# Second layers of expert pairs on four 32-column tiles of TensorE, gathers first, other weight buffers: attention and mixture of experts on one core

## The chip, the core and the metric

One core of a Trainium2 chip runs the whole program. The metric is the device time of one execution in microseconds (us), less is better. TensorE (PE) multiplies, VectorE (DVE) and ScalarE (ACT) work on rows in the on-chip memory and read the products out of PSUM, GpSimd (POOL) issues the indirect DMAs, and SyncE (SP) issues the plain DMAs of this stage. All DMAs of the core share 16 DMA engines.

## The reference

Attention with normalised queries and keys makes 3584 rows of 768 numbers. A gate picks one of 8 experts for each row, each expert keeps at most 80 rows, and those go through two layers. All other rows of the output are zero.

```python
q_n, k_n = rmsnorm(q, g_q), rmsnorm(k, g_k)        # batch 8, heads 12, seq 448, head_dim 64
attn = softmax(q_n @ k_n.T / 8);  x = attn @ v     # as (3584, 768)
logits = x @ w_gate                                # 8 experts
expert_idx = argmax(logits);  gate_w = softmax(logits)[expert_idx]
for e in range(8):
    tok_idx = the rows with expert_idx == e, the 80 of largest gate_w if there are more
    h = np.maximum(x[tok_idx] @ w1[e], 0.0)        # 768 x 1024
    out[tok_idx] = gate_w[tok_idx, None] * (h @ w2[e])   # 1024 x 768
```

## The kernel before

**Attention.** The 96 heads are done in 24 groups of four. Scores (L408) and products with v (L425) run on PE as four 64x64 tiles of the array at once, in f32, in an order written out by hand as slots. The gate's sums (L460) run as eight tiles of 64 rows by 32 columns. While this goes on, POOL copies the weights of experts 3 to 7 into a scratch in DRAM as bf16 (`stage_w`), and loads those of experts 0 to 2 on the chip.

**Late weights.** Near the end of attention SP begins to load the weights of experts 3 to 5 from the scratch into the memory that attention gives back (`weights_early`, `weights_late`, `fetch_late`). A weight tile that lies over a buffer of attention waits until that buffer has been read for the last time. Of expert 5, w1 is issued after the routing of the last batch has begun (L919 and the line behind it: a small memset holds it back), and w2 when the first gathered rows are there (L1023, again a memset that holds it back). Experts 6 and 7 go into the slots of experts 0 and 1 when PE is done with those (last two lines). SP works through its list in order, so a transfer that waits holds those behind it.

**Routing of the last batch.** DVE, PE and ACT find which rows each expert keeps, up to the indices `idxG`. PE fills its pauses with products that nobody reads (`busy`).

**Experts.** `gather(e)` fetches 80 rows by an indirect DMA. There are four row buffers, so gathers 0 to 3 are issued at once and gather e + 4 after the rows of e have been used. `xpose(e)` divides the rows by their softmax sums (three DVE products, L1017), transposes them on PE (six, L1027) and copies them out (DVE, L1030). The first layer is 48 matmuls with w1 as the stationary operand and 80 columns moving (L1045), and ACT's Relu (L1049). The second layer is 16 matmuls with 80 columns of h stationary and 384 columns of w2 moving (L1076): 8 chunks of the hidden size times two halves of the output. DVE weights the two halves (L1082) and POOL scatters the 80 rows to the output (L1064). The experts follow each other on PE, each as first layer, transposes of the next expert's rows, second layer. The last expert's output goes out in two scatters.

Of the kernel before, what the change touches and what calls it, by code (L numbers as in the profile page):

```python
# [21 lines left out]
def kernel(  # L22
# [154 lines left out]
    beat = tpool.tile([128, NJ + 1, 512], BF16, name="beat")  # L177
# [69 lines left out]
    vpool = av_stack.enter_context(tc.tile_pool(name="vp", bufs=3))  # L247
    apool = av_stack.enter_context(tc.tile_pool(name="attn", bufs=6))
    qktpool = av_stack.enter_context(tc.tile_pool(name="qkT", bufs=2))
    smpool = av_stack.enter_context(tc.tile_pool(name="sm", bufs=4))  # L250
    with av_stack:
# [24 lines left out]
        def load_v(g):  # L276
            vt = vpool.tile([128, NB, D], F32, tag="v", name="vt")
            load(g, vt, v, nc.sync)
            st[g]["v"] = vt
# [67 lines left out]
        def keys_turned(n):  # L347
# [5 lines left out]
            T = qktpool.tile([128, 2, S], F32, tag="qkT1", name="qkT")  # L353
# [26 lines left out]
        def transp(g, a):  # L380
# [6 lines left out]
            T = qktpool.tile([128, 2, S], F32, tag=f"qkT{a}", name="qkT")  # L387
# [531 lines left out]
    nc.vector.memset(w_tiles[NW0 + 2][0][0][:, 0, 0:2], 0.0)  # L919
    fetch_late(NW0 + 2, (0, ))  # L920
# [61 lines left out]
    def gather(e, wait=False):  # L982

        if e % 4 == 3:
            xgs[e] = prep.tile([128, NJ + 1, 256], F32, tag="xb", name="xg")[
                :CAP].rearrange("p j d -> p (j d)")[:, :XW]
        else:
            xgs[e] = upool.tile([128, 2, S], F32, tag="us", name="xg")[:CAP].rearrange(
                "p u s -> p (u s)")[:, :XW]
        if wait:  # L990
            nc.vector.memset(xgs[e][:, 0:1], 0.0)
        nc.gpsimd.indirect_dma_start(
            out=xgs[e], out_offset=None, in_=xr_dram[:, :],
# [18 lines left out]
    def xpose(e):  # L1012
        xg = xgs[e]
        xn = mpool.tile([CAP, DM], BF16, tag="xn", name="xn")
        for i in range(NQ):
            c = slice(256 * i, 256 * i + 256)
            nc.vector.tensor_mul(  # L1017
                xn[:, c].rearrange("p (hh u d) -> p u hh d", hh=2, u=2),
# [3 lines left out]
            if e == 0 and i == 0:  # L1022
                nc.vector.memset(w_tiles[NW0 + 2][1][0][:, 0, 0:2], 0.0)  # L1023
                fetch_late(NW0 + 2, (1, ))
        pxt = mps.tile([128, DC, CAP], BF16, tag="pxt", name="pxt", bufs=1)
        for c in range(DC):
            nc.tensor.transpose(pxt[:, c, :], xn[:, c * 128:(c + 1) * 128],  # L1027
                                identb[:CAP, :CAP])
        xgT = mpool.tile([128, DC, CAP], BF16, tag="xgT", name="xgT")
        nc.vector.tensor_copy(xgT[:], pxt[:])  # L1030
        xts[e] = xgT

    for e in range(1, 4):
        gather(e)
    xpose(0)

    busy(2)
    for e in range(E):
        h_sb = mpool.tile([128, FC, CAP], BF16, tag="hsb", name="h_sb")
        for fh in range(2):  # L1040
            ph = mps.tile([128, FC // 2, CAP], F32, tag="ph", name="ph")
            for f4 in range(FC // 2):
                fc = fh * (FC // 2) + f4
                for c in range(DC):
# [4 lines left out]
            nc.scalar.activation(h_sb[:, fh * (FC // 2):(fh + 1) * (FC // 2), :],  # L1049
                                 ph[:], AF.Relu)  # L1050
        if e + 1 < E:
            xpose(e + 1)
        if e < E - 4:
            gather(e + 4, wait=True)
        DN = DM // 2
        yo = mpool.tile([CAP, DM], F32, tag="yo", name="yo", bufs=3)

        def scatter(half=None):
            if half is None:
                o, at, y, n = outs[e], idxT[:, e:e + 1], yo[:, :], N  # L1060
            else:
                o = outs[e + half].rearrange("n (h d) -> (n h) d", h=2)
                at, y, n = idxL[:, half:half + 1], yo[:, half * DN:half * DN + DN], 2 * N
            nc.gpsimd.indirect_dma_start(  # L1064
                out=o[:, :], out_offset=bass.IndirectOffsetOnAxis(ap=at, axis=0),
# [77 lines left out]
```

## Time and profile before

| | us |
|---|---|
| three runs | 414.49, 417.03, 416.99 |
| median of them | 416.99 |
| profiled execution, its own time | 414.97 |
| span of its trace, first to last instruction | 413.3 |
| PE busy | 398.7 (96%) |
| DVE busy | 355.3 (86%) |
| ACT busy | 314.0 (76%) |
| attention and routing, up to the first matmul of an expert | 370.8 |
| experts, from there to the end | 42.5 |

The span is cut from the first to the last instruction of the program, so the execution's own time is 1.67 us more. Busy times are sums over the whole span, and the stages have different limits: what the table says of PE as a whole doesn't say what bounds the last 42.5 us.

### The profile page before, as it was taken

Reading aid. Unit: us, or ns where it says so; the run is one execution under the profiler, and the core shown is the slowest. Engines: PE = TensorE matmul, PEld = TensorE weight load, DVE = VectorE, ACT = ScalarE, POOL = GpSimd, SP = SyncE. Lnnn points to the kernel's source line nnn. Section 1 sums busy time; section 2 is a strip of 40 time slices with the busy share of each in tenths; the row PEclk is TensorE's granted clock in tenths of the full one; section 3 lists DMA queues with packets and bytes.
Section 4 is the critical chain, followed back from the end, with each engine's and each line's share of the span. In section 5 each row is a group of like instructions: output and inputs, shape, how many; then the busy total and the mean of one; then the engine's idle time right before and its main releaser. Section 6 shows DMA issues by size and latency. Waiting matters only on the chain.

```text
span 413.3 us, 12608 instructions
## 1 busy us (share of the span) xinstructions
PE 398.7 (96%) x5293; PEld 195.6 (47%) x5293; DVE 355.3 (86%) x659; ACT 314.0 (76%) x480; POOL 88.8 (21%) x148
## 2 busy tenths in 40 slices
PE   8999999999999999999999999999999999889994
PEld 7344444444444445344444444444344443448883
DVE  4999887998999999988999999989999969745551
ACT  5898979997989799979899699978997784502211
POOL 6200002501040013221241025111502030134422
PEclk9999999999999999999999999999999999999999
DMA  7459999999989899989999999999899285989991
GB/s 240 142 157 210 274 305 231 272 209 304 253 222 275 230 251 277 290 183 255 244 290 247 229 271 257 268 227 303 210 231 299 58 309 195 253 237 341 355 315 48
DMA packets 76072, 100.92 MB, mean 244 GB/s; under 512 B 8416, under 2 KB 65248, under 8 KB 76016
## 3 DMA queue, kind: packets, MB, share of 16 engines
q1 hardware_dynamic: 59856, 70.53, 53.2%
q0 software_dynamic: 15872, 29.13, 38.7%
q8 instruction: 41, 0.67, 0.6%
q10 hardware_dynamic: 288, 0.46, 0.4%
q14 instruction: 15, 0.12, 0.1%
HBM read 101.11 MB, written 39.89 MB: 341 GB/s over the span
## 4 chain that ended last, share of the span: by engine, by line
PE 84%; DVE 5%; ACT 5%; issue 2%; POOL 1%; DMA 1%; POOLq 0%; DVEq 0%
PE ps L408 31%; PE po L425 28%; PE zl L460 5%; PE py L1076 5%; PE tp L366 4%; PE ph L1045 4%; PE xp L366 3%; ACT at L411 1%; DVE sm L443 1%; DVE qn L329 1%; DVE ms L299 1%; DMA xg<-xr_scratch,idxG 1%; PE mp L638 1%; ACT zsb L470 1%; ACT zo L472 1%
## 5 line engine op out<-in xcount | busy, mean ns | idle before, releaser
L408 PE MATMUL ps<-qkT 64*64 64x448 f32 x1344 | 147.6, 548 | 2.8 <-ACT row L592 1.3
L411 ACT ACTIVATE at<-ps 128x896 f32<-128x896 f32 x168 | 146.5, 930 | 4.5 <-PE ps L408 3.3
L425 PE MATMUL po<-at,vt 64*64 64x448 f32 x1344 | 142.5, 537 | 0.0
L443 DVE TENSOR_TENSOR sm<-sm,at 128x896 f32<-128x896 f32 x120 | 130.5, 1088 | 3.1
L425 PEld LDWEIGHTS po<-at,vt 64*64 64x64 f32 x1344 | 50.0, 133 | 74.0 <-issue 63.9
L408 PEld LDWEIGHTS ps<-qkT 64*64 64x64 f32 x1344 | 43.5, 132 | 67.5 <-issue 26.3
L299 DVE TENSOR_REDUCE ms<-sq 128x14 f32<-128x896 f32 (+1 forms) x50 | 51.9, 1041 | 7.1 <-ACT sq L292 7.0
L329 DVE TENSOR_TENSOR qn<-qk,rs 128x896 f32<-128x896 f32 (+1 forms) x47 | 50.5, 1077 | 1.6 <-issue 0.3
L292 ACT ACTIVATE sq<-qk 128x896 f32<-128x896 f32 (+1 forms) x48 | 44.5, 930 | 2.1 <-DMA qk<-in_q_dram 2.1
L216 POOL COPY mark<-mark 1x1 bf16<-1x1 bf16 x22 | 7.9, 359 | 138.9 <-DVE mark L215 138.9
L1049 ACT ACTIVATE h_sb<-ph 128x320 bf16<-128x320 f32 x16 | 7.0, 438 | 38.0 <-PE ph L1045 32.4
L705 ACT COPY xb<-xp 128x1024 f32<-128x1024 f32 x24 | 24.3, 1012 | 8.8 <-PE xp L366 8.4
L366 PEld LDWEIGHTS tp<-ident,qn 64*128 64x128 f32 x672 | 23.5, 139 | 12.6 <-issue 4.4
L366 PE MATMUL tp<-ident,qn 64*128 64x64 f32 x672 | 27.1, 226 | 0.6 <-POOL qn L329 0.4
L432 ACT COPY us<-po 128x896 f32<-128x896 f32 (+1 forms) x24 | 21.4, 894 | 6.5 <-PE po L425 6.4
L441 DVE TENSOR_TENSOR sm<-at 128x896 f32<-128x896 f32 x24 | 26.0, 1083 | 0.1
L395 ACT ACTIVATE qkT<-tp,gqk 128x896 f32<-128x896 f32 x23 | 23.6, 1026 | 0.0
L397 ACT COPY qkT<-tp 128x896 f32<-128x896 f32 x24 | 22.0, 916 | 2.0 <-PE tp L366 2.0
L1076 PE MATMUL py<-w_sb,h_sb 128*80 128x384 bf16 (+1 forms) x136 | 22.4, 317 | 0.1
L460 PE MATMUL zl<-us,wgs 64*32 64x448 f32 x192 | 20.4, 540 | 0.0
L460 PE MATMUL zl<-sm,zsel 64*32 64x448 f32 x192 | 20.3, 540 | 0.0
L366 PEld LDWEIGHTS xp<-ident,us 64*128 64x128 f32 x384 | 14.0, 139 | 12.0 <-ACT at L411 10.6
(185 smaller groups left out, 426.0 us busy)
## 6 DMA issues: line engine op xcount, KB each, us to landing
wb_scratch<-in_moe_w_dram POOLq DMA_DIRECT2D x20, 768.0 KB, 10.2
w_sb<-wb_scratch SPq DMA_DIRECT2D x9, 1536.0 KB, 13.6
vt<-in_v_dram SPq DMA_DIRECT2D x24, 448.0 KB, 6.5
out_dram<-zeros SPq DMA_DIRECT2D x28, 384.0 KB, 6.5
qk<-in_q_dram SPq DMA_DIRECT2D x23, 448.0 KB, 7.3
qk<-in_k_dram SPq DMA_DIRECT2D x23, 448.0 KB, 5.5
w_sb<-in_moe_w_dram POOLq DMA_DIRECT2D x6, 1536.0 KB, 15.7
xr_scratch<-xb SPq DMA_DIRECT2D x48, 192.0 KB, 7.1
```

The source lines that it names most:

```text
L292: nc.scalar.activation(o, x, AF.Square)
L299: nc.vector.reduce_sum(out=st[g]["ms"][:, a, lo:hi], in_=st[g]["sq%d" % a][:, lo:hi], axis=AX.X)
L329: e.tensor_mul(qn[:].rearrange("p (x hh) d -> p hh x d", hh=2)[:, h0:h1], qk[:, lo:hi].rearrange("p (hh x) d -> p hh x d", x=NX), rs[:, lo ...
L366: nc.tensor.transpose(o, w, one[p, p], tile_position=(p.start, 0))
L408: nc.tensor.matmul(ps[u * 64:u * 64 + 64, hh, :S], T1[d, u, x * 64:(x + 1) * 64], T0[d, u, :], start=True, stop=True)
L411: nc.scalar.activation(at[:], ps[:, :, :S], AF.Exp)
L425: nc.tensor.matmul(po[u][hh * D:(hh + 1) * D, u, :S], vt[p, hh * NX + x, :], at[p, hh, :], start=(x == 0), stop=(x == RD - 1))
L441: nc.vector.tensor_add(s["sm"][:], s["at0"][:], s["at1"][:])
L443: nc.vector.tensor_add(s["sm"][:], s["sm"][:], s["at%d" % x][:])
L460: nc.tensor.matmul(t[32 * c:32 * c + 32, r, :S], w, x, start=(i == 0), stop=(i == NQ - 1))
L705: nc.scalar.copy(xb[:].rearrange("p j (u hh d) -> p hh (j u) d", u=2, hh=2), xp[:].rearrange("p hh (k d) -> p hh k d", d=D))
L1076: nc.tensor.matmul(py[:, :c1 - c0], h_sb[:, fc, :], chunk(e, 1, fc)[:, c0:c1], start=(fc == 0), stop=(fc == FC - 1))
```

## The change

Four things change in the expert stage, and one in the layout of memory. Expert 0 and expert 7 keep their second layer. Experts 1 to 6 go in pairs (1,2), (3,4), (5,6): both first layers, then `second_layers`. That makes three products of 384 columns, each into one PSUM bank: the 80 rows of one half of one expert's output as column tiles of 32, 32 and 16 columns of the array at PSUM partitions 0 to 79, and in the fourth column tile, at partitions 96 and up, a third of the rows of the fourth half (expert b, second half). ACT weights what is in the fourth tile, with a copy of the gate weights at those partitions (`gwL`). There are six row buffers: gathers 0 to 5 are issued at once, and gathers 6 and 7 right after the rows of experts 0 and 1 have been divided. The division (`normal`) is issued two experts ahead of use, in `turn_rows(e)` for expert e + 2. Expert 7's slot is refilled after the second layers of the pair (1,2). The buffers of attention are laid out so that w2 of expert 4 lies over buffers of the last group but one, and w1 of expert 5 is issued in `weights_late` without a memset.

```diff
-    vpool = av_stack.enter_context(tc.tile_pool(name="vp", bufs=3))
+    vpools, qktpools = [], []
+    for last in range(2):
+        vpools.append(av_stack.enter_context(tc.tile_pool(name=f"vp{last}", bufs=2 - last)))
+        qktpools.append(av_stack.enter_context(tc.tile_pool(name=f"qkT{last}", bufs=1)))
...
             fetch_late(NW0 + 1)
+            fetch_late(NW0 + 2, (0, ))
...
-    nc.vector.memset(w_tiles[NW0 + 2][0][0][:, 0, 0:2], 0.0)
-    fetch_late(NW0 + 2, (0, ))
...
+    def gather(e):
+        if e == 5:
+            t = tpool.tile([128, XW], F32, tag="beat", name="xg")[:CAP]
+        elif e in (3, 4):
+            t = prep.tile([128, NJ + 1, 256], F32, tag="xb", name="xg")[
...
+    def turn_rows(e):
         pxt = mps.tile([128, DC, CAP], BF16, tag="pxt", name="pxt", bufs=1)
...
+        xts[e] = mpool.tile([128, DC, CAP], BF16, tag="xgT", name="xgT")
+        nc.vector.tensor_copy(xts[e][:], pxt[:])
+        if e + 2 < E and e:
+            normal(e + 2)
...
+    TB = [slice(32 * t, min(32 * t + 32, CAP)) for t in range(3)]
+    lasts = [slice(96, 96 + t.stop - t.start) for t in TB]
+    def second_layers(a, b):
+        rows_of(a)
+        rows_of(b)
+        for k, (e, half) in enumerate(((a, 0), (a, 1), (b, 0))):
+            py = product(k)
+            last = lasts[k]
+            for fc in range(FC):
+                for p in TB:
+                    nc.tensor.matmul(py[p, :], hs[e][:, fc, p],
+                                     chunk(e, 1, fc)[:, half * DN:half * DN + DN],
+                                     start=(fc == 0), stop=(fc == FC - 1))
+                nc.tensor.matmul(py[last, :], hs[b][:, fc, TB[k]], chunk(b, 1, fc)[:, DN:],
+                                 start=(fc == 0), stop=(fc == FC - 1))
+            weighted(yos[e][:, half * DN:half * DN + DN], py[:CAP, :], gwT[:, e:e + 1], False)
+            weighted(yos[b][TB[k], DN:], py[last, :], gwL[last, k, b:b + 1], True)
+            if k:
+                scatter(e)
+
+    for e in range(1, 6):
+        gather(e)
+    normal(0)
+    turn_rows(0)
+    normal(1)
+    normal(2)
+    for e in range(6, E):
+        gather(e)
+    busy(2)
+    first_layer(0)
...
+    turn_rows(1)
+    second_layer(0, lambda: turn_rows(2))
+    refill(0)
+    for a in range(1, E - 1, 2):
+        first_layer(a)
+        turn_rows(a + 2)
+        first_layer(a + 1)
+        if a + 3 < E:
+            turn_rows(a + 3)
+        second_layers(a, a + 1)
+        if a == 1:
+            refill(1)
+    first_layer(E - 1)
+    second_layer(E - 1)
```

The order of DVE, from the division of expert 0's rows to the weighting of expert 1's output. `xn` are divided rows, `xgT` transposed ones, `yo` weighted output. Before:

```order
L1017 TENSOR_TENSOR xn<-xg 80x2x2x64 x2
L1030 COPY xgT<-pxt 128x480
L1017 TENSOR_TENSOR xn<-xg 80x2x2x64 x3
L1030 COPY xgT<-pxt 128x480
L991 MEMSET xg 80x1
L1082 TENSOR_SCALAR yo<-py,gwT 80x384 x2
L1017 TENSOR_TENSOR xn<-xg 80x2x2x64 x3
L1030 COPY xgT<-pxt 128x480
L991 MEMSET xg 80x1
L1082 TENSOR_SCALAR yo<-py,gwT 80x384 x2
```

The same engine and place with the change, up to the copy of expert 4's rows:

```order
L1021 TENSOR_TENSOR xn_5807<-xg_5763 80x2x2x64 x2
L1036 COPY xgT_5820<-pxt_5813 128x480
L1021 TENSOR_TENSOR xn_5822<-xg_5797 80x2x2x64 x3
L1021 TENSOR_TENSOR xn_5826<-xg_5799 80x2x2x64 x3
L1036 COPY xgT_5899<-pxt_5892 128x480
L1021 TENSOR_TENSOR xn_5901<-xg_5801 80x2x2x64 x3
L1036 COPY xgT_5923<-pxt_5916 128x480
L1021 TENSOR_TENSOR xn_5925<-xg_5803 80x2x2x64 x3
L1084 TENSOR_SCALAR yo_5905<-py_5906,gwT_5767 80x384
L1084 TENSOR_SCALAR yo_5905<-py_5907,gwT_5767 80x384
L1036 COPY xgT_6006<-pxt_5999 128x480
L1021 TENSOR_TENSOR xn_6008<-xg_5805 80x2x2x64 x3
```

The divisions of experts 2, 3 and 4 now stand ahead of the weighting of expert 0, and each division (xg_5799 is gather 2, xg_5801 gather 3, xg_5803 gather 4, xg_5805 gather 5) stands ahead of the copy of the transposed rows of an earlier expert.

The list of SP from the last w1 part of expert 4 to the end. `xb` and `rz` are the attention's rows and their softmax sums on the way to DRAM, where the gathers read them. Before:

```order
L231 DMA w_sb<-wb_scratch 128x1024
L229 DMA w_sb<-wb_scratch 128x8x768
L717 DMA xr_scratch<-xb 64x3x256 x2
...
L509 DMA xr_scratch<-rz 64x3x12
L229 DMA w_sb<-wb_scratch 128x6x1024
L229 DMA w_sb<-wb_scratch 128x8x768
L229 DMA w_sb<-wb_scratch 128x6x1024
L229 DMA w_sb<-wb_scratch 128x8x768
L229 DMA w_sb<-wb_scratch 128x6x1024
L229 DMA w_sb<-wb_scratch 128x8x768
```

The same list with the change:

```order
L231 DMA w_sb<-wb_scratch 128x1024
L229 DMA w_sb<-wb_scratch 128x8x768
L229 DMA w_sb<-wb_scratch 128x6x1024
L719 DMA xr_scratch<-xb 64x3x256 x2
...
L511 DMA xr_scratch<-rz 64x3x12
L229 DMA w_sb<-wb_scratch 128x8x768
L229 DMA w_sb<-wb_scratch 128x6x1024
L229 DMA w_sb<-wb_scratch 128x8x768
L229 DMA w_sb<-wb_scratch 128x6x1024
L229 DMA w_sb<-wb_scratch 128x8x768
```

One transfer has moved, w1 of expert 5 (128x6x1024): it stands ahead of the last rows of attention now and no longer behind the last softmax sums. The five behind it (w2 of expert 5, then w1 and w2 of experts 6 and 7) keep their order.

## Rows read from the trace of the kernel before

**Rows 1.** Busy time by stretch: PE, PEld, DVE, ACT, POOL, clock, DMA share, GB/s

```profile
366.00:371.00 5.00, 4.18 (x28) 1.78 (x26) 1.81 (x6) 0.00 (x0) 3.20 (x4) 1.00 0.68 179
371.00:401.00 30.00, 30.00 (x479) 25.22 (x477) 17.02 (x44) 6.08 (x14) 10.63 (x10) 1.00 1.04 347
401.00:402.00 1.00, 1.00 (x8) 0.73 (x7) 0.10 (x1) 0.05 (x1) 0.00 (x0) 1.00 0.67 212
402.00:403.00 1.00, 1.00 (x13) 0.75 (x12) 0.66 (x2) 0.00 (x0) 0.00 (x0) 1.00 0.11 45
```

**Rows 2.** The chain of work that ended last, in the expert stage: start, us

```profile
365.41 3.42 DMA xg<-xr_scratch,idxG
370.80 1.88 PE ph L1045 x48
372.90 2.60 PE py L1076 x16
375.50 1.72 PE ph L1045 x48
```

**Rows 3.** Timeline of PE over the experts: start, us, count

```profile
372.52 0.38 PE L1027 MATMUL pxt<-identb,xn 80*128 80x80 bf16 x6
372.74 2.77 PE L1076 MATMUL py<-w_sb,h_sb 128*80 128x384 bf16 x16
375.34 1.88 PE L1045 MATMUL ph<-xgT,w_sb 128*128 128x80 bf16 x48
...
402.76 1.88 PE L1045 MATMUL ph<-xgT,w_sb 128*128 128x80 bf16 x48
404.48 3.07 PE L1076 MATMUL py<-w_sb,h_sb 128*80 128x384 bf16 x24
```

**Rows 4.** Timeline of PE at the gate's sums, first matmul of two batches

```profile
348.36 0.54 PE L460 MATMUL zl<-sm,zsel 64*32 64x448 f32 x1
...
348.73 0.54 PE L460 MATMUL zl<-sm,zsel 64*32 64x448 f32 x1
```

**Rows 5.** Timeline of PE at the start: f32 on the whole array

```profile
6.23 1.91 PE L852 MATMUL wps<-zeros 128*128 128x192 f32 x10
```

**Rows 6.** Timeline of SP: w2 of expert 4, w1 and w2 of 5

```profile
351.44 0.37 SPq L229 DMA_DIRECT2D w_sb<-wb_scratch  x1
359.50 0.48 SPq L229 DMA_DIRECT2D w_sb<-wb_scratch  x1
369.32 0.36 SPq L229 DMA_DIRECT2D w_sb<-wb_scratch  x1
```

**Rows 7.** Timeline of POOL: gathers 2 and 3, scatter of expert 5

```profile
368.01 0.90 POOL L992 DMA_INDIRECT xg<-xr_scratch,idxG  x1 [0.30 <-issue]
369.21 0.90 POOL L992 DMA_INDIRECT xg<-xr_scratch,idxG  x1 [0.30 <-issue]
...
399.22 0.91 POOL L1064 DMA_INDIRECT out_dram<-yo,idxT  x1 [3.35 <-DVE yo L1082]
```

**Rows 8.** DMA issues, gathers 3 and 4: the last number is us to landing

```profile
xg<-xr_scratch,idxG POOLq DMA_INDIRECT x1, 7.5
xg<-xr_scratch,idxG POOLq DMA_INDIRECT x1, 7.9
```

**Rows 9.** Timeline of DVE: experts 0 and 1, division of expert 3's rows

```profile
370.67 1.08 DVE L1017 TENSOR_TENSOR xn<-xg 80x256 bf16<-80x256 f32 x3
372.94 0.41 DVE L1030 COPY xgT<-pxt 128x480 bf16<-128x480 bf16 x1 [1.19 <-PE pxt L1027]
...
374.89 1.26 DVE L1082 TENSOR_SCALAR yo<-py,gwT 80x384 f32<-80x384 f32 x2 [1.54 <-PE py L1076]
...
380.63 1.08 DVE L1017 TENSOR_TENSOR xn<-xg 80x256 bf16<-80x256 f32 x3
```

**Rows 10.** Timeline of SP and DMA issues: w2 of expert 7, us to landing

```profile
382.27 4.47 SPq L229 DMA_DIRECT2D w_sb<-wb_scratch  x1
...
w_sb<-wb_scratch SPq DMA_DIRECT2D x1, 1536.0 KB, 20.3
```

More of the change, by code (lines that the diff above doesn't have):

```diff
@@ L175 @@
                             compare_op=ALU.is_gt, fill=0.0, base=0, channel_multiplier=-1)
-    beat = tpool.tile([128, NJ + 1, 512], BF16, name="beat")
+    beat = tpool.tile([128, NJ + 1, 512], BF16, tag="beat", name="beat")
     tied = tpool.tile([128, NJ + 1, 128], BF16, name="tied")
@@ L276, in load_v @@
         def load_v(g):
[L277 removed]
+            vt = vpools[g % 3 == (NG - 1) % 3].tile([128, NB, D], F32, tag="v", name="vt")
             load(g, vt, v, nc.sync)
@@ L1048 @@
                                      start=(c == 0), stop=(c == DC - 1))
[L1049 to L1065, printed above, removed]
-                in_=y, in_offset=None, bounds_check=n - 1, oob_is_err=False)
@@ L1068 @@
-        cuts = (0, DN, DM) if e + 1 < E else (0, DN, DN + DN // 2, DM)
-        pys = [(mps.tile([CAP, DN], F32, tag="py" if i < 2 else "pz", name="py",
-                         bufs=2 if i < 2 else 1), c0, c1)
-               for i, (c0, c1) in enumerate(zip(cuts, cuts[1:]))]
-        def product(p, fcs):
-            py, c0, c1 = p
-            for fc in fcs:
-                nc.tensor.matmul(py[:, :c1 - c0], h_sb[:, fc, :], chunk(e, 1, fc)[:, c0:c1],
-                                 start=(fc == 0), stop=(fc == FC - 1))
@@ L1079, in weighted @@
[L1079 to L1104 removed]
+            nc.scalar.activation(hs[e][:, fh * HC:(fh + 1) * HC, :], ph[:], AF.Relu)
@@ L1105, with refill @@
+    def refill(e):
         if NW0 + 3 + e < E:
@@ L1107, with weighted, second_layer, sums @@
             fetch_late(NW0 + 3 + e)
+    def weighted(o, x, w, late):
+        if late:
+            nc.scalar.activation(o, x, AF.Copy, scale=w)
+        else:
+            nc.vector.tensor_scalar(o, x, w, None, op0=ALU.mult)
+    def second_layer(e, between=None):
+        rows_of(e)
+        cuts = (0, DN, DM) if e + 1 < E else (0, DN, DN + DN // 2, DM)
+        pys = [(product(i), c0, c1) for i, (c0, c1) in enumerate(zip(cuts, cuts[1:]))]
+        def sums(i, fcs):
+            py, c0, c1 = pys[i]
+            for fc in fcs:
+                nc.tensor.matmul(py[:CAP, :c1 - c0], hs[e][:, fc, :], chunk(e, 1, fc)[:, c0:c1],
+                                 start=(fc == 0), stop=(fc == FC - 1))
+        def done(i):
+            py, c0, c1 = pys[i]
+            weighted(yos[e][:, c0:c1], py[:CAP, :c1 - c0], gwT[:, e:e + 1], i > 1)
+        for fh in range(2):
+            for i in range(2):
+                sums(i, range(fh * HC, fh * HC + HC))
+            if fh == 0 and between is not None:
+                between()
+        done(0)
+        if len(pys) == 2:
+            done(1)
+            scatter(e)
+            return
+        scatter(e, 0)
+        sums(2, range(FC))
+        done(1)
+        done(2)
+        scatter(e, 1)
@@ new lines @@
+    for e in range(1, 6):
[8 more added lines that the diff above has]
+    first_layer(0)
+    for k in range(3):
+        nc.scalar.copy(gwL[lasts[k], k, :], gwT[TB[k], :])
+    turn_rows(1)
[10 more added lines that the diff above has]
+            refill(1)
```

85 lines of the change are left out of this document (35 added, 50 removed).

## The prediction

> **What bounds the kernel now.** I read the page's engine table first and set it aside: the change touches the last 42.5 us, so the stage has to be read by itself. Busy time by stretch [rows 1] shows that stage in one line: from 371 to 401 us PE is busy 30.00 of 30.00 us, and the DMA engines stand at a share of 1.04 with 347 GB/s. Two resources are full side by side. The chain of waits [rows 2] tells which one ends last: from 370.80 on it names PE alone, first layers of 1.72 us and second layers of 2.60 us (1.88 for the very first). Before that stands the landing of the first gather, 3.42 us from its issue. On the timeline of PE [rows 3] the experts come at a fixed beat: a first layer begins at 375.34, the last expert's at 402.76, six periods of 4.57 us later. No expert waits for a weight. So PE is the bound, with DMA close behind, and the question is how close.
>
> It is very close. The last weight, w2 of expert 7, is issued at 382.27 and lands 20.3 us later [rows 10], at 402.6. The stretches agree: DMA share 0.67 from 401 to 402, 0.11 in the next microsecond [rows 1]. PE begins to use it at 404.48 [rows 3]. The slack is 1.9 us. Whatever PE gains beyond that in front of this point is waited for there, unless the transfer also comes earlier.
>
> **The change part by part.**
>
> *Column tiles.* A pair's second layers take 2 x 2.60 = 5.20 us now, 32 matmuls of 384 columns at 0.1625 us [rows 2]. Afterwards there are three products of 8 chunks, each chunk a batch of four matmuls in four column tiles. The trace has no bf16 matmul of 128 rows on column tiles. From below, a batch costs what one matmul of 384 columns costs, 0.1625 us. From above I take the only four-column tiling in the trace, the gate's sums: eight tiles of 64x32, whose batches of 448 f32 columns start 0.37 us apart [rows 4], 0.84 ns a column, which makes 0.32 us for 384. But that is f32: on the whole array ten f32 matmuls of 192 columns take 1.91 us [rows 5], 0.9 to 1.0 ns a column. A column costs f32 as much without tiles, so tiling cost nothing there, though each of the four column tiles has weights and moving data of its own. I take the lower end: 24 x 0.1625 = 3.90 us a pair, 1.30 saved, three pairs 3.90 us. At the upper end a pair costs 7.70 and the three lose 7.5. Issue is no limit: the first layer issues 48 pairs of load and matmul in 1.72 us, 36 ns each [rows 2], and four pairs in 0.1625 us need 41 ns each.
>
> *Weighting.* DVE's three products of a pair replace four, ACT gets three of 16 or 32 rows. Both engines have room (17.02 and 6.08 of 30 us [rows 1]), and a first layer of 1.72 us lies between one use of a PSUM bank and the next. Nothing, and at most one such product (0.6 us, half of the pair in [rows 9]) before the last expert.
>
> *Gathers first.* Six issues stand in a row on POOL, 1.2 us apart [rows 7], so gather 4 comes at 370.4 and gather 5 at 371.6, neither of which waits for a row buffer any more. The division now runs two experts ahead on DVE, which takes its list in order. Gather 3 is issued at 369.21 as before and needs 7.5 us, gather 4 needed 7.9 [rows 8], because the DMA engines are full from 371 on. In the kernel before nobody noticed: gather 3 was used at 380.63 [rows 9]. Now the division of expert 3 stands ahead of the copy of expert 2's transposed rows, and that of expert 4 ahead of the weighting of expert 0 and the copy of expert 3. I walk it through with durations from [rows 9], taking 7.5 us per gather:
> gather 3 lands at 376.7, division to 377.8, copy of expert 2 to 378.2. PE, which has 0.22 us more of transposes in expert 0's second layer [rows 3], ends the first layer of expert 1 at 375.56 + 1.72 = 377.28 and wants the one PSUM buffer for the transposes of expert 3; it is free at 378.2. Wait: 0.9 us. First layer of expert 2 to 380.1. On DVE: gather 4 landed at 377.9, division to 379.3, weighting of expert 0 to 380.5, copy of expert 3 to 380.9, and only then may PE transpose expert 4's rows. Wait: 0.8 us. Gather 5 is there at 379.1, and behind it nothing holds PE any more. Sum 1.7 us. From below this is zero (gathers that land as quickly as the first one, 3.42 us [rows 2]). From above each gather stands 4.1 us (7.5 less 3.42) behind the one ahead of it: then gather 4 lands at 380.8, 5 at 384.9, 6 at 389.0, the first pair waits 4.3 us, and the next one another 1.1 because the weighting stands behind the division of gather 6; 5.4 us. I take 1.7, since all of these are queued within 4 us and 7.5 is what such a gather needed.
>
> *Late weights.* In the list of SP only w1 of expert 5 moves. w2 of expert 4, issued at 351.44 [rows 6], waited for the last product of attention; it may now go as soon as the last group but one is through, and w1 of expert 5 takes its place ahead of attention's last rows. Those rows and the gathers behind them see one transfer of the same size as before. What is freed is the time of w1 of expert 5, issued at 359.50 [rows 6]. Nobody waited for it, and the next transfer, w2 of expert 5, is still held until the rows of expert 0 have been divided, 369.32 [rows 6]. From there on the same five weights, gathers and scatters stand in the queue, so the landing at 402.6 hardly moves. One thing is less: of the six scatters issued by 399.22 [rows 7] the last comes about a microsecond later than before. It is 80 rows of 3 KB, 0.25 MB, 0.7 us at 347 GB/s, of which about half stood ahead of the weight. Landing: 402.2, between 401.5 and 403.0. Expert 7's refill is issued later (after the first pair, about 385), but before SP already stood on that issue for 4.47 us [rows 10], until 386.7, with the queue full: no cost. The first gather may land a little sooner, 0 to 0.4 us; I take 0.
>
> *Sum.* The last second layer begins, by PE, at 404.48 - 3.90 + 1.7 = 402.3; by the weights at 402.2 and a tenth. The later one counts: 402.3. What follows (8.8 us, to 413.3) is the same code. The gain is 2.2 us: span 411.1, execution 412.8 against the profiled 414.97.
>
> The runs shown lie at 414.49 and at 417.0 twice, the profiled one near the lower. I take the gain from the middle between the profiled time and the median, 416.0, and forecast 413.8. A measurement of this kernel can tell about 1%, 4.2 us, from no change.
>
> **The rivals.**
> 1. *Neither limit bites*: the gathers land before DVE asks, and the weights come sooner than the queue says. Then all 3.90 us and perhaps 0.3 of the first gather are seen: about 411.9. For it speaks that the stretch from 366 to 371 has a share of 0.68 [rows 1], room for the early gathers; against it that w2 of expert 5 starts into just that room.
> 2. *The gathers queue up* in front of DVE. Price up to 5.4 us as worked out, so between the forecast and 404.48 - 3.90 + 5.4, which is 1.5 us slower: 417.5. It turns to a loss from 3.9 us of waits on.
> 3. *The column tiles overlap only in part*, the slower side: with b us per batch of four the end moves by 72b - 15.6 + 1.7. It loses from b = 0.193 on; at f32's rate, 0.32, it is 9.1 us slower, 425.1. Rows 4 and 5 speak against it as said, but only in f32. The Trainium skill has a rule on this side ("TensorE: Matmul & The Clock Gate", "Measured speedup vs the span model"): three column tiles of 32 with 512 columns ran 2.38 times as fast as one after another, not 3 times. By that a batch would cost 0.1625 x 3 / 2.38 = 0.205 us, an estimate from that page, and the kernel would be 0.9 us slower, 416.9; the trace's gate sums don't show such a loss.
> 4. *The layout doesn't do what it says*, w2 of expert 4 still waits for the end of attention. Then w1 of expert 5 lands one such transfer later, still far ahead of its use: no change to the forecast.
>
> **How the numbers follow.** Forecast, both limits near 402: 0.53. Rival 1: 0.22. Rival 2 beyond the forecast's 1.7 us: 0.15. Rival 3: 0.10, half of it over 1%. Rival 4 lies within the first. The range runs from rival 1 taken from the lower of the runs' levels (411.2) to rival 2's and the skill's end (416.9). Faster by over 1% (under 412.8): most of rival 1's better half and about a quarter of the forecast, since the level of the runs can hide or add 1 us: 0.27. Slower by over 1%: 0.06. Within: 0.67.
>
> **What would show it.** Right: batches of four matmuls 0.16 us apart, a pair's second layers in 3.9 us; PE waiting for DVE ahead of the transposes of experts 3 and 4; w2 of expert 7 landing near 402 and PE idle or just arriving there. Wrong, if PE never waits after 372 us, if w2 of expert 7 lands before 401, if batches of four are over 0.19 us apart, or if the first gather lands more than half a microsecond away from 368.8.

## The result, and the profile after

| | before | after |
|---|---|---|
| median, us | 416.92 (9 runs, 414.49 to 417.24) | 418.58 (9 runs, 417.51 to 419.86) |
| ratio, 95% interval | | 1.0058, 1.0035 to 1.0081 |
| profiled execution, its own time and span, us | 414.97, 413.3 | 419.86, 418.2 |

The change doesn't gain 2.2 us, it loses 1.7. That is within the 1% that a measurement of this kernel can tell, but the interval lies above 1, and 418.58 is above the range of the prediction. The timeline of PE over the experts, after (start, us, what, count; in brackets the idle time before it and what ended it):

```profile
371.02 1.88 PE L1051 MATMUL ph<-xgT,w_sb 128*128 128x80 bf16 x48
...
375.77 1.88 PE L1051 MATMUL ph<-xgT,w_sb 128*128 128x80 bf16 x48
379.44 0.38 PE L1033 MATMUL pxt<-identb,xn 80*128 80x80 bf16 x6 [1.78 <-DVE xgT L1036]
...
384.03 0.38 PE L1033 MATMUL pxt<-identb,xn 80*128 80x80 bf16 x6 [2.49 <-DVE xgT L1036]
384.33 0.34 PE L1130 MATMUL py<-w_sb,h_sb 128*32 128x384 bf16 x3
384.34 0.34 PE L1133 MATMUL py<-w_sb,h_sb 128*32 128x384 bf16 x1
384.50 0.33 PE L1130 MATMUL py<-w_sb,h_sb 128*32 128x384 bf16 x3
...
388.35 1.61 PE L1051 MATMUL ph<-xgT,w_sb 128*128 128x80 bf16 x40
390.16 0.45 PE L1051 MATMUL ph<-xgT,w_sb 128*128 128x80 bf16 x8 [0.20 <-issue]
...
396.63 0.34 PE L1130 MATMUL py<-w_sb,h_sb 128*32 128x384 bf16 x3 [1.32 <-issue]
...
398.21 1.89 PE L1051 MATMUL ph<-xgT,w_sb 128*128 128x80 bf16 x48
399.94 0.38 PE L1033 MATMUL pxt<-identb,xn 80*128 80x80 bf16 x6
400.15 1.53 PE L1051 MATMUL ph<-xgT,w_sb 128*128 128x80 bf16 x38
403.10 0.52 PE L1051 MATMUL ph<-xgT,w_sb 128*128 128x80 bf16 x10 [1.42 <-issue]
...
407.56 1.89 PE L1051 MATMUL ph<-xgT,w_sb 128*128 128x80 bf16 x48
409.48 2.81 PE L1094 MATMUL py<-w_sb,h_sb 128*80 128x384 bf16 x24
```

The tiles work: batches of four start 0.17 us apart (384.33, 384.50), and a pair's second layers take 4.0 us (384.33 to 388.35). But PE, which waited for nothing before [rows 1], now idles in two ways: 1.78 and 2.49 us for VectorE ahead of the transposes of experts 3 and 4, and 0.20, 1.32 and 1.42 us for nothing that the profile shows ("issue"). The last expert's first layer starts at 407.56, not at 402.76 [rows 3], 4.8 us later. The brackets count from the modelled end of a matmul, 0.17 us after the next one could have begun, so I take the account from start to start: second layers of the pairs -3.6 (4.0 us each, without the gaps, for 5.2), waits for VectorE +4.6 (1.95 and 2.66), gaps +3.5 (0.37, 1.49 and 1.68), a later start of expert 1 +0.4 (375.77 for 375.34), transposes -0.2. That is 4.7 of the 4.8 us. It holds for the two profiled executions, which lie 4.9 us apart, the changed one being the slowest of its nine; the medians lie 1.7 us apart, and how much of each part the other executions have isn't recorded.

The timeline of DVE there, which in [rows 9] had the division of expert 3 at 380.63 and no wait ahead of it:

```profile
377.98 1.09 DVE L1021 TENSOR_TENSOR xn<-xg 80x256 bf16<-80x256 f32 x3 [4.41 <-DMA xg<-xr_scratch,idxG]
378.99 0.40 DVE L1036 COPY xgT<-pxt 128x480 bf16<-128x480 bf16 x1
381.52 1.09 DVE L1021 TENSOR_TENSOR xn<-xg 80x256 bf16<-80x256 f32 x3 [2.13 <-DMA xg<-xr_scratch,idxG]
382.53 1.13 DVE L1084 TENSOR_SCALAR yo<-py,gwT 80x384 f32<-80x384 f32 x2
383.58 0.39 DVE L1036 COPY xgT<-pxt 128x480 bf16<-128x480 bf16 x1
```

VectorE stands 4.41 us in front of gather 3 and 2.13 us in front of gather 4, and the copies that PE needs stand behind it in its list. The DMA issues of 368 to 371 us, after (last number: us to landing; [rows 8] had 7.5 and 7.9):

```profile
w_sb<-wb_scratch SPq DMA_DIRECT2D x1, 1536.0 KB, 16.0
xg<-xr_scratch,idxG POOLq DMA_INDIRECT x3, 8.7
```

The end of the late weights, by stretches after (columns as in [rows 1]):

```profile
401.00:402.00 1.00, 0.68 (x20) 0.58 (x17) 0.00 (x0) 0.44 (x1) 0.00 (x0) 1.00 0.95 312
402.00:403.00 1.00, 0.00 (x0) 0.00 (x0) 0.00 (x0) 0.00 (x0) 0.00 (x0) 1.00 0.39 152
403.00:404.00 1.00, 0.90 (x22) 0.72 (x25) 0.00 (x0) 0.34 (x1) 0.00 (x0) 1.00 0.12 48
```

The DMA engines go quiet about 1 us later than before (share 0.12 from 403 on, not from 402 [rows 1]). Nobody waits for that: expert 7's first layer only starts at 407.56.

### The profile page after: what moved, and what is told of

Same layout as the page of the kernel before. It is cut to its first block, busy times and chain, and to the rows that moved or that the text cites. A ratio compares the mean times of both kernels' runs of the same rounds, so it can differ in the third digit from the quotient of the medians.

```text
span 418.2 us, 12996 instructions
## 1 busy us (share of the span) xinstructions
PE 396.5 (95%) x5485; PEld 192.8 (46%) x5485; DVE 352.6 (84%) x651; ACT 319.6 (76%) x492; POOL 87.6 (21%) x148
## 4 chain that ended last, share of the span: by engine, by line
PE 82%; DVE 6%; ACT 5%; DMA 3%; issue 2%; POOLq 0%; POOL 0%; DVEq 0%
PE ps L410 31%; PE po L427 28%; PE zl L462 5%; PE tp L368 4%; DMA xg<-xr_scratch,idxG 3%; PE xp L368 3%; PE py L1130 3%; PE ph L1051 2%; PE wps L855 2%; ACT at L413 1%; DVE sm L445 1%; DVE qn L331 1%; DVE ms L301 1%; PE mp L640 1%; ACT zsb L472 1%
## 5 line engine op out<-in xcount | busy, mean ns | idle before, releaser
L1084 DVE TENSOR_SCALAR yo<-py,gwT 80x384 f32<-80x384 f32 (+1 forms) x13 | 7.6, 596 | 13.7 <-PE py L1133 10.7
```

## The experiments

Two theories stood at first. **G**: gathers 3 and 4 land late because w2 of expert 5 (1.5 MB, issued at 369.6) takes the DMA engines beside them, and VectorE, in order, hands the wait on to PE. **I**: the gaps without a releaser are PE running out of instructions. Two rows of the page after:

```profile
PE 396.5 (95%) x5485; PEld 192.8 (46%) x5485; DVE 352.6 (84%) x651; ACT 319.6 (76%) x492; POOL 87.6 (21%) x148
...
q8 instruction: 43, 0.70, 0.6%
```

PE has 10970 matmuls and loads and queue q8 moved 43 packets, one for 255 of them (before: 10586 and 41, one for 258), which fits a queue that feeds PE. The tiles issue eight instructions in 0.16 us where one matmul and its load stood before. In the DMA views from 394.0 to 395.3 and from 400.5 to 401.7 us, the ends of the last stretches in which PE worked before its two long gaps, there is one such packet each; from 388 to 394 there is none:

```profile
q8 instruction: 1, 0.02, 5.4%
...
q8 instruction: 1, 0.02, 5.8%
```

The Trainium skill ("Runtime: NRT & Kernel Launch", "Instruction fetch mechanics") says that instructions come in blocks of 16 KiB, 256 of them, through a DMA queue of the sequencer's own, and that crossing a block is mostly hidden. The count agrees; whether it is hidden here is what I asked. The gaps stand one such block apart. From 396.63 to 403.10 PE runs nine batches of four matmuls, then 48, 6 and 38: 128 matmuls with their 128 loads, 256 instructions. From 390.16 to 396.63 it is 128 and 128 again. Both stretches last 6.47 us, and PE works for about 5.1 of them. In quarters of a microsecond of the DMA view the packets begin at 387.5, 394.0, 400.5 and 404.5 (within 0.25 us). Each of the three gaps ends 2.4 to 2.7 us after one of them. The next packet comes 3.8 to 4.1 us after a gap has ended while the DMA engines stand at a share of over 1, and 1.4 to 1.7 us after the last gap, where the share is 0.12; no gap follows that one. The rival of I: PE loses the time in switching between tiled and whole-array matmuls.

The runs stand in five groups, each on one chip with runs of the kernel before.

### Group 1 (before: 416.48): which part costs

**w2_early** issues w2 of expert 5 before the first gather, without the hold:

```diff
     gate2p(b)
+    fetch_late(NW0 + 2, (1, ))
...
-            if e == 0 and i == 0:
-                nc.vector.memset(w_tiles[NW0 + 2][1][0][:, 0, 0:2], 0.0)
-                fetch_late(NW0 + 2, (1, ))
```

> The changed kernel, with w2 of expert 5 issued after the last softmax sums (where the kernel before issued w1 of expert 5) and not held back until the first rows are there. Theory G (the 1.5 MB of w2 of expert 5 start just ahead of gathers 3 to 5 in the DMA engines, these land late, and the order on VectorE passes the delay on to the transposes): the waits of TensorE ahead of the transposes of experts 3 and 4, 4.3 us in the changed kernel, fall under 0.5 us, gather 3 lands within 4 us, w2 of expert 7 lands 4 us earlier (near 400), and the time is 4 us under the changed kernel, about 414.5. Theory I (TensorE's instructions, fetched in blocks of 16 KB, come late while the DMA engines are full): the gaps of 1.3 to 1.4 us without a releaser stay, two of them. Rival (the order on VectorE alone makes the waits, however early gathers land): waits of over 3 us stay, time over 417.5.

Measured: 415.96, ratio 0.9996 (0.9968 to 1.0024). Its timeline of PE:

```profile
370.51 0.92 PE L1031 MATMUL pxt<-identb,xn 80*128 80x80 bf16 x6 [1.96 <-DVE xn L1022]
...
371.93 3.23 PE L1049 MATMUL ph<-xgT,w_sb 128*128 128x80 bf16 x48
...
379.98 0.38 PE L1031 MATMUL pxt<-identb,xn 80*128 80x80 bf16 x6
...
381.92 0.38 PE L1031 MATMUL pxt<-identb,xn 80*128 80x80 bf16 x6
...
394.21 0.34 PE L1128 MATMUL py<-w_sb,h_sb 128*32 128x384 bf16 x3 [1.31 <-issue]
```

Its stretch from 372 to 376 us:

```profile
372.00:376.00 4.00, 4.00 (x58) 3.85 (x58) 2.28 (x8) 1.19 (x4) 2.24 (x3) 0.57 0.82 211
```

The waits ahead of the transposes of experts 3 and 4 (379.98, 381.92) are gone, and not only because PE comes later: gather 4, issued at 370.15, is divided from 377.49 without a wait, so it needed 7.3 us at most, for 10.9 in the changed kernel. G holds. Its time was forecast at 414.5, with two gaps; there is one. The price moved to the front. The first gather lands later behind the weights, PE idles 1.96 us, and the first layer that follows takes 3.23 us at a granted clock of 0.57 of 2.4 GHz, near the lower level of 1.2, for 1.88 us at 1.00 in the changed kernel. Together with a gap of 1.31 that eats the gain.

**tiles_only** keeps the pairs and goes back to the gathers, divisions and four row buffers of before:

```diff
-        if e + 2 < E and e:
-            normal(e + 2)
...
+        xpose(a + 1)
+        if a + 4 < E:
+            gather(a + 4, wait=True)
```

> The changed kernel with the gathers, row buffers and divisions of the kernel before (four buffers, one division ahead of its transposes), so column tiles and layout alone. G: no wait over 0.5 us ahead of the transposes; I: gaps of TensorE without a releaser of 1 us or more stay, 1 to 3 us in all; then the last second layer begins at 402 to 403.5 and the time is 1 to 2.5 us under the kernel before, ratio 0.994 to 0.998. If the gathers are not the cause of the loss: ratio over 1.003.

Measured: 417.47, 1.0022 (1.0000 to 1.0044), between the two forecasts. Gaps without a releaser of 1.38 and 0.63 us, three waits for VectorE of 0.59 us each, and behind gap and wait together (387.24 to 388.29) a first layer of 3.36 us, at a granted clock of 0.57 from 388 to 392. The tiles alone gain nothing either.

**gathers_only** keeps the gathers and goes back to one expert after the other:

```diff
+    for e in range(E):
+        first_layer(e)
+        if e + 1 < E:
+            turn_rows(e + 1)
+        second_layer(e)
+        refill(e)
```

> The changed kernel without pairs: every expert has its second layer of 16 whole-array matmuls right after its first, gathers, divisions two ahead and layout as in the change. G: the weighting of expert 0 stands behind the division of expert 3 on VectorE, whose gather lands near 377.5, so the second layer of expert 1 waits about 2 us for its PSUM bank and the kernel is 2 us slower than before (ratio 1.005); later experts wait for nothing. I: no gap of over 0.5 us without a releaser, since instructions are used as slowly as before. If the gathers first cost nothing by themselves: ratio 0.999 to 1.001.

Measured: 416.76, 1.0027 (0.9998 to 1.0056). VectorE waits 3.85 us for gather 3, and PE waits 1.43 us for a PSUM bank whose weighting stands behind that division. There is no gap without a releaser. G forecast some 2 us more than before (1.005); the interval just includes 1, no change.

**quarters** is the kernel before, with no tiles, and each matmul of a second layer cut into four of 96 columns:

```diff
+                for o in range(0, c1 - c0, 96):
+                    nc.tensor.matmul(py[:, o:o + 96], h_sb[:, fc, :],
```

> The kernel before, each matmul of a second layer split into four of 96 columns on the whole array, so four times the instructions there for nearly the same work of TensorE (0.1 us more per expert, 0.9 in all), no column tiles, gathers as before. Theory I: some 236 instructions in 4.6 us instead of 140, so gaps without a releaser of about 1.4 us appear after 375 us, two or more, and the time is 1.5 to 4 us over the kernel before. Rival (the gaps belong to column tiling, a change of the array's mode): no such gap, at most 1.2 us over before.

Measured: 423.27, 1.0148 (1.0096 to 1.0201). Its timeline of PE:

```profile
387.69 1.64 PE L1077 MATMUL py<-w_sb,h_sb 128*80 128x96 bf16 x34 [1.23 <-issue]
389.17 1.88 PE L1045 MATMUL ph<-xgT,w_sb 128*128 128x80 bf16 x48
390.89 0.41 PE L1027 MATMUL pxt<-identb,xn 80*128 80x80 bf16 x6
391.15 1.82 PE L1077 MATMUL py<-w_sb,h_sb 128*80 128x96 bf16 x39
394.34 1.26 PE L1077 MATMUL py<-w_sb,h_sb 128*80 128x96 bf16 x25 [1.37 <-issue]
...
400.87 0.84 PE L1077 MATMUL py<-w_sb,h_sb 128*80 128x96 bf16 x16 [1.26 <-issue]
```

The same gaps without any tile, with four times the instructions in the second layers: the rival of I falls. From gap to gap there are 127 matmuls (34, 48, 6 and 39, and as many in the next stretch), one short of a block. The loss is larger than the 1.5 to 4 us of the forecast, and part of it stands ahead of the first cut matmul: the first transposes come at 370.89 for 369.33, behind 2.31 us of idle, and the first layer behind them takes 3.26 us at a granted clock of 0.58. Why the first gather was later in this profile isn't shown.

### Group 2 (before: 415.91)

**late_turns** transposes the next pair's rows after the first and second product of a pair and divides behind the weighting, so that no late gather stands ahead of what PE needs; **both** adds w2_early to it.

```diff
-        turn_rows(a + 2)
...
+        second_layers(a, a + 1, (a + 2, a + 3))
+        for e in (a + 4, a + 5):
+            if e < E:
+                normal(e)
```

> The changed kernel, with the transposes of the next pair's rows moved behind the first and second product of a pair's second layers, and the divisions behind the weighting on VectorE; w2 of expert 5 held as in the change. Theory G: gathers land as late as in the changed kernel (gather 4 near 381.5), but nothing that TensorE wants by then stands behind them, so the 4.3 us of waits ahead of transposes fall under 1 us; gaps for instructions (theory I) stay, 2 to 3 us. The landing of w2 of expert 7, about 403.5, is the next limit, so the time is that of before less 0 to 1 us: 415.5 to 417.

> The late transposes and the early w2 of expert 5 together. G: no wait ahead of transposes; w2 of expert 7 lands near 399 and is not waited for. I: gaps for instructions of 1.3 to 1.6 us remain, one to three. Without them the last second layer would begin at 400.7, with two of them at 403.5: 412.5 to 416, best of the kernels so far.

Measured: 420.89, 1.0117 (1.0086 to 1.0147), and 421.47, 1.0131 (1.0100 to 1.0161). The waits ahead of the transposes are gone in both, and yet they are slower than before and slower than forecast. Something new had come: in the first layer of expert 0 PE stops after 36 matmuls in late_turns (37 in both), and until 376.5 us only one to three come every 0.7 us or so. I call it the crawl; its rows stand in group 4.

**quiet** is w2_early without the loads for experts 6 and 7, which use the weights of 0 and 1 (the output of two experts differs):

```diff
-            load_weights(wpool, NW0 + 3 + e, e)
-            fetch_late(NW0 + 3 + e)
+            w_tiles[NW0 + 3 + e] = w_tiles[e]
```

> The early w2 of expert 5, and no weights for experts 6 and 7 (they use those of experts 0 and 1, so the output of two experts differs): after 373 us the DMA engines carry gathers and scatters alone. Theory I: the gaps without a releaser vanish (under 0.4 us each), the last second layer begins at 400.7 plus at most 0.5, time about 412.5 to 413.5. Rival (the gaps come from column tiles or from the number of instructions whatever the DMA load): the gaps of 1.3 us stay and the time is over 414.5.

Measured: 418.59, 1.0058 (1.0033 to 1.0083), with the crawl, so the time of 412.5 to 413.5 wasn't reached. Behind it, by stretches:

```profile
384.00:394.00 10.00, 10.00 (x257) 8.17 (x254) 5.27 (x13) 4.24 (x9) 2.79 (x3) 1.00 0.19 53
394.00:404.00 10.00, 10.00 (x258) 8.10 (x258) 3.45 (x8) 4.31 (x9) 1.82 (x3) 1.00 0.27 77
```

With the DMA engines at a share of 0.19 and 0.27, PE runs the same pairs without a gap for 20 us. In the changed kernel the share was 1.03 and 0.95 in the microsecond in which each of the two long gaps began. This is what theory I expects: PE goes through a block of 128 matmuls and loads in 5.0 us here and doesn't stop.

### Group 3 (before: 416.78)

**three_tiles** has two column tiles for an expert's 80 rows (64 and 16 columns) instead of three; **early_fill** is w2_early with 25 products that nobody reads ahead of the first gather instead of 18; **early_fill_three** is both; **quiet_again** is quiet, unaltered.

```diff
-                for p in TB:
+                for p in (slice(0, 64), TB[2]):
...
-    busy(18)
+    busy(25)
```

> The changed kernel, with the three column tiles of one expert's 80 rows (32, 32, 16 columns) replaced by two (64 and 16): three matmuls a batch instead of four, the same columns streamed, the same results. PE's instructions in a pair of second layers fall from 192 loads and matmuls to 144 of them. If the gaps of 1.3 and 1.4 us without a releaser in the changed kernel come from PE using up its instructions faster than blocks of 256 of them arrive (theory I), a block lasts 6.9 us instead of 5.2 in the pairs and the two gaps shrink to under 0.5 us each: about 416.5 us. If they belong to something else (the switch between tiled and whole-array matmuls, or a wait that the profile doesn't name), they stay, and the time is that of the changed kernel, 418.5. The waits of 1.8 and 2.5 us ahead of the transposes of experts 3 and 4 stay in both.

> The changed kernel with w2 of expert 5 issued before the first gather's rows are there (as in w2_early), and 25 instead of 18 products that nobody reads while the first gather is under way (0.22 us each, so PE idles some 0.4 us instead of 1.96 ahead of the transposes of expert 0). If the half clock in the first layer of expert 0 follows from that idle time, the clock stays at 1.0 from 371 to 376, the first layer takes 1.9 us instead of 3.23 and the kernel gains 1.4 us on w2_early: about 414.6. If the clock falls for another reason, or the longer filler makes the transposes late, it stays at 416.

> early_fill and three_tiles together. By theory G (waits for late gathers gone), the clock kept up, and theory I (no gap without a releaser in the pairs), the account is: kernel before, less 3.9 us for the tiles, plus 1.5 us for the first gather that lands later behind the weights: 414.4, ratio to before 0.994. If theory I is wrong a gap of 1.3 us stays and it is 415 to 416.

> The same kernel as quiet (experts 6 and 7 use the weights of 0 and 1, so nothing is loaded behind w2 of expert 5, and two experts' output differs). If the crawl of PE in the first layer of expert 0, single matmuls 0.7 us apart from 373 to 377, belongs to the chip or the moment, it is gone here and the time is 3 to 5 us less than 418.6: about 414. If it belongs to the program (where its instructions lie), it is there again: 418.6.

Measured: 444.94, 1.0682 (1.0651 to 1.0712); 419.75, 1.0085 (1.0054 to 1.0116); 445.45, 1.0686 (1.0653 to 1.0719); 417.80, 1.0029 (1.0005 to 1.0052). All four crawl. Fewer instructions didn't help, for a reason of its own, on the timeline of PE of three_tiles:

```profile
385.38 0.61 PE L1130 MATMUL py<-w_sb,h_sb 128*64 128x384 bf16 x2
385.67 0.34 PE L1133 MATMUL py<-w_sb,h_sb 128*32 128x384 bf16 x1
385.93 0.61 PE L1130 MATMUL py<-w_sb,h_sb 128*64 128x384 bf16 x2
```

A batch of three takes 0.55 us (385.38 to 385.93), more than three matmuls on the whole array one after another (0.49): with tiles of 64 and of 32 columns side by side nothing is gained. As a test of I it says nothing. Nor does early_fill speak on the clock as meant: PE idled only 0.24 us ahead of the transposes, but then the crawl came, and the clock fell to 0.67 behind that. quiet_again crawls from 373 to 376.4 at a DMA share of 0.72 to 0.78, and late_turns at 1.09, so full DMA engines aren't needed for it.

### Group 4 (before: 416.00): is it the chip

**after_again** is the changed kernel and **early_again** is w2_early, both unaltered. **early_awake** and **after_awake** are the two with ScalarE's copies of the gate weights ahead of its first Relu, since its first Relu came 16.2 us after its last work in the crawls seen till then.

```diff
+    for k in range(3):
+        nc.scalar.copy(gwL[lasts[k], k, :], gwT[TB[k], :])
     for e in range(1, 6):
         gather(e)
```

> The changed kernel, unaltered, beside the three kernels below on one chip. If the crawl of PE in the first layer of expert 0 (single matmuls 0.7 us apart until 16.2 us after ScalarE's last instruction, seen in late_turns, quiet, early_fill and three_tiles) belongs to the chip, it can show up here too, and the time is 420 to 422; if it belongs to those programs, the first layer takes 1.9 us as before and the time is 418.5.

> w2_early, unaltered. It ran without the crawl on the first chip (415.96) and with PE code like that of quiet, which crawled on two others. If the crawl belongs to the chip, it is here when it is in after_again, and costs 3 to 4 us: 419 to 420. Otherwise 416, with no wait ahead of the transposes of experts 3 and 4 once more.

> w2_early with ScalarE's three small copies of the gate weights placed ahead of its first Relu, so that ScalarE has work at about 368 us and is not idle for 11 to 16 us before the first layer of expert 0. If the crawl comes from ScalarE's long idle time, it is absent here even where early_again has it: 416. If it comes from PE or the chip, it is as in early_again.

> The changed kernel with the same move of ScalarE's three copies. Without a crawl in after_again no difference: 418.5, waits of 1.8 and 2.5 us ahead of the transposes of experts 3 and 4, and gaps of some 1.3 us without a releaser in the pairs. With a crawl there and none here, the copies have removed it, 2 to 3 us less than after_again.

Measured: 420.79, 1.0122 (1.0087 to 1.0157); 420.67, 1.0093 (1.0056 to 1.0129); 420.34, 1.0109 (1.0075 to 1.0144); 420.07, 1.0106 (1.0069 to 1.0142). All crawl. The timeline of PE of after_again, to hold against the first fence above:

```profile
370.61 1.45 PE L1051 MATMUL ph<-xgT,w_sb 128*128 128x80 bf16 x36
372.25 0.20 PE L1051 MATMUL ph<-xgT,w_sb 128*128 128x80 bf16 x1 [0.19 <-issue]
372.97 0.20 PE L1051 MATMUL ph<-xgT,w_sb 128*128 128x80 bf16 x1 [0.53 <-issue]
373.69 0.28 PE L1051 MATMUL ph<-xgT,w_sb 128*128 128x80 bf16 x3 [0.52 <-issue]
...
376.57 0.36 PE L1051 MATMUL ph<-xgT,w_sb 128*128 128x80 bf16 x3 [1.15 <-issue]
376.73 0.60 PE L1033 MATMUL pxt<-identb,xn 80*128 80x80 bf16 x6
377.17 2.78 PE L1094 MATMUL py<-w_sb,h_sb 128*80 128x384 bf16 x8
```

The stretch from 376 to 380 us, and behind it the last gather of GpSimd's list:

```profile
376.00:380.00 4.00, 3.42 (x21) 2.31 (x21) 1.41 (x4) 1.35 (x5) 0.00 (x0) 0.50 1.04 230
```

```profile
374.00 0.90 POOL L994 DMA_INDIRECT xg<-xr_scratch,idxG  x1 [0.30 <-issue]
```

The same program that ran its first layer in 1.88 us needs 6.3 us here (370.61 to 376.93), and then goes on at a clock of 0.50. It doesn't look like a late block, since queue q8 moves no packet from 366 to 380 us here. So the crawl depends on the chip or the moment (each group ran on one chip, so the two can't be told apart), and it is part of what the change costs, since the kernel before keeps its time in all five groups (415.39 to 416.78). ScalarE's idle time isn't its cause: in early_awake ScalarE had worked at 364.9, and it crawled. What stood out was GpSimd: its list of eight gathers, four before, ends at 374.90 here, and the crawl 1.7 us later.

### Group 5 (before: 415.39): GpSimd's list

**after_third** is the changed kernel, **gathers_again** is gathers_only, both unaltered. **after_split** holds gathers 6 and 7 back until the weighting of expert 0, by a memset of a column of their row buffers:

```diff
-    for e in range(6, E):
-        gather(e)
...
     second_layer(0, lambda: turn_rows(2))
+    for e in range(6, E):
+        gather(e, wait=True)
```

> The changed kernel, unaltered, as the control of this chip: 418.5 with a first layer of expert 0 of 1.9 us (no crawl), or 420.8 with one that crawls from 372 to 376.6 us. Only in the second case do the other two kernels of this chip tell anything of the crawl.

> The changed kernel with gathers 6 and 7 held back until the weighting of expert 0 (a memset of one column of their row buffers on VectorE, behind it), so that GpSimd's first list has six gathers and ends at about 372.4 us instead of 374.9. In nine crawling profiles the crawl ended 1.5 to 1.9 us after the last gather of that list. If the list of gathers is what slows PE's sequencer, the crawl ends at 374 to 374.3 here and the kernel is 2.3 us faster than after_third on the same chip. If the crawl only happens to end then, it ends at 376.5 here too, and the two kernels agree.

> gathers_only, unaltered: no column tiles, but the six row buffers and the eight gathers in one list. It ran without a crawl on the first chip (416.76). If the crawl goes with the gathers (or the chip), it is here when it is in after_third, and the time is 419 to 420; if it needs the longer PE program of the column tiles, it isn't: 416.8.

Measured: 420.34, 1.0111 (1.0068 to 1.0154); 423.23, 1.0172 (1.0132 to 1.0212); 421.26, 1.0131 (1.0091 to 1.0170). Both unaltered kernels crawl until 376.5. The timeline of PE of after_split:

```profile
370.43 1.82 PE L1053 MATMUL ph<-xgT,w_sb 128*128 128x80 bf16 x40
373.40 0.45 PE L1053 MATMUL ph<-xgT,w_sb 128*128 128x80 bf16 x8 [1.15 <-issue]
...
381.78 0.56 PE L1035 MATMUL pxt<-identb,xn 80*128 80x80 bf16 x6 [3.01 <-DVE xgT L1038]
```

And its last gather of GpSimd's first list:

```profile
371.23 0.91 POOL L996 DMA_INDIRECT xg<-xr_scratch,idxG  x1 [0.30 <-issue]
```

The list ends 2.8 us sooner (372.14), and the crawl, here a single stop, ends 3.1 us sooner, 1.3 us behind it; full speed is back at 373.40, and the clock is 1.00 until 377. That the end of the list of gathers sets the end of the crawl is so far borne out, by one profile; that gathers_again crawls says that it needs no tile. The list alone isn't enough: with the same eight gathers in a row the first profile of the change, w2_early and gathers_only have no crawl. tiles_only, with four, ran on no chip that crawled. The forecast of the time failed: the kernel is 2.9 us slower than after_third, because PE, no longer held up, now waits 3.01 us for gather 3 (divided from 380.31), as G has it, and later for the gathers that were held back (from 392 to 396 us it is busy for 1.15 of 4).

## Why the prediction was wrong

Two steps failed: instructions were said to be no limit, and the wait for the late gathers was taken too small. Where the crawl comes, a cost stands beside them that no step had.

- **Column tiles**: right. 0.1625 us a batch was taken, 0.16 to 0.17 is what the timeline shows, 4.0 us a pair for 3.90. Rival 3 falls, and with it the rule of the Trainium skill ("TensorE: Matmul & The Clock Gate", "Measured speedup vs the span model") that would have made 0.205, as an estimate: four tiles of up to 32 columns ran side by side at the price of one matmul.
- **"Issue is no limit"**: this step failed. It weighed the rate at which PE takes instructions (36 ns for a pair of them against 41) and not where they come from. There is no term for it in the sum; it measured 3.5 us in the profile after. quarters shows that it goes with the number of instructions and not with tiles, quiet that it goes with full DMA engines. The gaps stand 256 instructions apart and each ends 2.4 to 2.7 us after a packet of q8: with the DMA engines full the next block could be used 6.5 us after the last one, and PE had used that up in about 5.1. In the kernel before the packets stand 8.0 us apart (377.0, 385.0, 393.0), and PE never stops. The profile doesn't name what a packet holds; that it is PE's instructions rests on these counts and times.
- **Gathers first**: the mechanism was right, and PE waited at the two places named. The size was off: 1.7 us were taken, 4.6 measured from start to start, a little over the upper bound's 4.3 for the first pair. The sum took 7.5 us per gather "since all of these are queued within 4 us"; gather 3 needed 8.8 (issued at 369.17, divided from 377.98), gather 4 10.9 (370.61, 381.52), 3.5 us behind it. The gathers line up behind each other, as in the upper bound (4.1 us), and behind w2 of expert 5. Rival 2 named this at 0.15. Its point, a loss from 3.9 us of waits on, was reached. The range didn't hold its own rival: its upper end, 416.9, lies below the 417.5 that rival 2 was worked out to, and the measured 418.58 lies above both.
- **What the gathers cost PE elsewhere**: no step and no rival had the crawl. On two chips it hits the unaltered changed kernel, and ratios of 1.0122 and 1.0111 stand where the first measurement gave 1.0058. In after_third it makes expert 0's first layer and the step to the second 6.3 us long (370.81 to 377.08) for 1.9 before, and the second layer, at half clock, 5.0 (to 382.10) for the 2.8 of the first profile. The waits for gathers 3 and 4 on PE (4.3 us) are hidden under it there, and of the gaps only one of 0.9 is left, so the spans are alike all the same (418.1 and 418.2).
- **Late weights**: they were no limit. The landing slipped to about 403 (402.2 was forecast), but PE came to the last second layer at 409.48, 7.2 us later than the forecast's 402.3, and not because of the weights.
- **Layout**: SP issues w2 of expert 4 at 341.08, for 351.44 before, so the layout did what it says and rival 4 falls; nothing in the first layers waits for a weight.

None of the versions beats the kernel before. w2_early in group 1 comes closest (0.9996), and on another chip it crawls too (1.0093). What stays open: whether and how GpSimd's gathers slow PE, and why one chip, or one moment, shows it and another doesn't. What drops the clock is open too. It fell behind an idle of PE in w2_early, tiles_only, quarters and the crawls, but in the first profile of the change PE idled 2.49 us ahead of 384.03, and the clock was 1.00 in the microsecond behind it. Filling the idle could not be tried without the crawl in the way.

## What to carry to other kernels

When PE works without a pause, count what feeds it, not only what it computes: four times the instructions for the same columns is a load on the instruction queue, which shares the DMA engines with the weights. Here a block of 256 instructions that PE used up in 5.1 us was followed by the next after 6.5. Work that is issued "early, since it is free" is issued onto something: eight gathers in a row cost 4.6 us here through VectorE's in-order list, and saved nothing on PE, which had waited for nothing before. Where the crawl came they cost more. And a term whose upper bound would turn the sign deserves the queue's arithmetic, not the duration of a like transfer in a calmer place.

## What was not expected of the hardware

- PE stands still for 1.2 to 1.4 us at a time without a releaser, every 256 of its instructions, where it uses these up in about 5.1 us and the DMA engines are at a share of 0.95 and more (the profile after, quarters); at a share of 0.19 to 0.27 it doesn't (quiet).
- Column tiles of 32 columns overlap four at a time (0.16 to 0.17 us a batch of 384 columns); with one of 64 columns beside a 16 and a 32 (three_tiles) a batch of three takes 0.55 us.
- While GpSimd works through its row of gathers, PE stops or falls to a few matmuls per 0.7 us, from between 372 and 374 until 376.2 to 377.0 us, in the profiles of 13 kernels of groups 2 to 5 with eight gathers in a row, and until 373.4 in the one with six; the end comes 1.3 to 1.9 us after the last of these gathers has been issued. In three profiles with eight gathers (the first one of the change, w2_early, gathers_only) it doesn't happen.
- The granted clock was between 0.50 and 0.67 from 376 to 380 us in the profiles with a crawl into that stretch, and 0.57 behind an idle of 1.96 us (w2_early); behind an idle of 2.49 us in the first profile of the change it was 1.00.
